# A retention kernel fused with an act-snake feed-forward layer: the first chunks interleaved, and work moved between GpSimd, VectorE and ScalarE

## The chip, the cores and the metric

The kernel runs on one core of a Trainium2 chip. The metric is the device time of one execution, in microseconds (us), and smaller is better. The runs shown of the kernel before are three, with a median of 246.03 us (245.74 to 247.08).

## What is computed

The reference has two steps. The first is a retention recurrence over q, k and v (batch 4, 8 heads, 768 positions, head width 64) with one decay `gamma` per head. The second takes the 3072 x 512 result x through a feed-forward layer of width 2048 with the activation h + sin(alpha h)^2 / alpha:

```python
for t in range(S):
    state = gamma * state + outer(k[t], v[t])
    y[t] = scale * q[t] @ state
x = y.transpose(0, 2, 1, 3).reshape(B * S, H * D)
h = x @ w_in
s = sin(alpha * h)
out = (h + s * s / (alpha + 1e-9)) @ w_out
```

## The kernel before, in words

**Tiling.** The recurrence is computed in 24 chunks of 128 positions (6 for each batch). A chunk j goes through four steps. `scale_v` (L163) multiplies v by decay powers `kg` into a new tile `vs`. `stage_T` (L168) transposes q and k on TensorE (PE) with eight transposes into the PSUM tile `pt`, and copies them to SBUF as `qkT`. `stage_A` (L181) makes the 128 x 128 products of k and q for the eight heads in the PSUM tile `pa`, and VectorE (DVE) multiplies them with a causal mask into `aT`. `stage_M` (L193), called the mix below, adds the product of the carried state `s_bd` and q to that of `vs` and `aT` in the PSUM tile `py`; DVE multiplies `py` with the decay table `qg` of the chunk's place into `xT` (L220), and ScalarE (ACT) copies the new state `ps` into `s_bd` (L224).

**Groups.** The 24 chunks form seven groups of 3, 2, 4, 4, 4, 4 and 3. For a group, `phase` (L309) runs through the 16 blocks f of the feed-forward width. `ff_in` (L229) multiplies block f of `w_in` with the group's `xT` into a PSUM tile `ph`; ACT takes the sine (L238); the square is made by ACT, DVE or GpSimd (POOL), by a pattern of the letters A, D and P (L240, L243); and DVE joins square and `ph` into `gT` (L244). Into the same loop are written, by hand, the steps T, A and M of the next group's chunks (the table `att`, by f) and the products of the group before with `w_out` (`ff_out`, L250, which accumulates 16 blocks in a PSUM tile `po`, copies it out at L262 and stores it). Below, phase 0 to phase 6 are these loops.

**Order.** The schedule is manual: each engine carries out its instructions in the order in which the program names them. All loads but three go through POOL's queue, cast from float32 to bfloat16 on the way. The program issues 14 of them ahead (L113), and the others one or three at a time out of the `att` tables. Between them POOL's queue has the decay tables (L149), `scale_v` from chunk 3 on (L165), and the squares of letter P (L243). The first q and k come in float32 through the sync engine's queue and are cast on DVE (L285, L286).

**PSUM.** There are eight banks. Four belong to the tag `mm` (`ph`, `po`, `scratch` and `pal`), two to `pa`, one to `ps`, and one to the tag `ty`, which `pt` and `py` share: the transposes of a chunk wait until `xT` of the chunk before has been read out of it.

**The start.** Before phase 0 the chunks 0, 1 and 2 run one after the other (L285 to L306), with matmuls on a tile of zeros (`idle_work`, L275) in the gaps. In `stage_T` with `split` the q half is copied by ACT (L175) and the k half by DVE (L176).

Of the kernel before, what the change touches and what calls it, by code (L numbers as in the profile page):

```python
# [15 lines left out]
def kernel(  # L16
# [56 lines left out]

    WP = 4
# [45 lines left out]
    mask01 = consts.tile([128, 128], BF16, name="mask01")  # L120
    nc.vector.tensor_scalar(mask01, tio, pos[:, 0:1], None, op0=ALU.is_ge)
    mask_bc = mask01[:, None, :].to_broadcast([128, H, 128])


# [6 lines left out]
    kg = consts.tile([128, NCH, H], F32, name="kg")  # L131
    nc.scalar.activation(out=kg, in_=expo, func=ACTF.Exp, scale=-1.0)

    lgp = consts.tile([128, NP], F32, name="lgp")
    for p in range(NP):
        for e in range(2):
            nc.vector.memset(lgp[64 * e:64 * e + 64, p:p + 1], lng[2 * p + e])
    qg = consts.tile([128, NCH, NP, C], F32, name="qg")
    for p in range(NP):
        nc.scalar.activation(out=qg[:, 0, p, :], in_=tio, func=ACTF.Exp, scale=lgp[:, p:p + 1])  # L140
    step = consts.tile([128, NCH, NP], F32, name="step")
    for c in range(1, NCH):
        nc.scalar.activation(out=step[:, c, :], in_=lgp, func=ACTF.Exp, scale=float(C * c))
    for name in "qk":
        raw[name, 0] = big.tile([128, H, D], BF16, name=f"{name}b")
    nc.vector.tensor_scalar_mul(qg[:, 0], qg[:, 0], scale)

    def decay_table(c, eng):
        eng.tensor_mul(qg[:, c], qg[:, 0], step[:, c, :, None].to_broadcast([128, NP, C]))  # L149


    s_bd = [big.tile([128, NP, 128], BF16, name=f"s_bd{i}") for i in range(2)]
    for t in s_bd:
        nc.vector.memset(t, 0.0)
# [178 lines left out]
    def L(n):  # L333
        return lambda: issue(n)
# [79 lines left out]
```

## Time and profile before

| | before |
|---|---|
| median of the runs | 246.03 us |
| the profiled execution's own time | 248.4 us |
| its span, first to last instruction | 246.4 us |
| PE busy | 217.8 us (88%) |
| DVE busy | 156.6 us (64%) |
| ACT busy | 148.1 us (60%) |
| POOL busy | 97.3 us (39%) |

Busy time is the time in which an engine works on an instruction; PEld is TensorE's loading of weights, which lies beside its matmuls. A row of a timeline gives start, duration, engine, line, operation and tiles, how many instructions were merged, and in brackets the idle time before it with what ended it. "PEclk" is the granted TensorE clock as a share of 2.4 GHz: 0.50 is the lower of its two levels, 1.2 GHz. A granted clock of 1.00 is also shown for stretches in which TensorE does nothing or has only begun.

### The profile page before, as it was taken

Reading aid. Unit: us, or ns where it says so; the run is one execution under the profiler, and the core shown is the slowest. Engines: PE = TensorE matmul, PEld = TensorE weight load, DVE = VectorE, ACT = ScalarE, POOL = GpSimd, SP = SyncE. Lnnn points to the kernel's source line nnn. Section 1 sums busy time; section 2 is a strip of 40 time slices with the busy share of each in tenths; the row PEclk is TensorE's granted clock in tenths of the full one; section 3 lists DMA queues with packets and bytes.
Section 4 is the critical chain, followed back from the end, with each engine's and each line's share of the span. In section 5 each row is a group of like instructions: output and inputs, shape, how many; then the busy total and the mean of one; then the engine's idle time right before and its main releaser. Section 6 shows DMA issues by size and latency. Waiting matters only on the chain.

```text
span 246.4 us, 4382 instructions
## 1 busy us (share of the span) xinstructions
PE 217.8 (88%) x1728; PEld 115.3 (47%) x1755; DVE 156.6 (64%) x247; ACT 148.1 (60%) x272; POOL 97.3 (39%) x112
## 2 busy tenths in 40 slices
PE   6786975798879989699999799999799999999993
PEld 2344543455654545344554444545444554555441
DVE  5655596458994787737766756876674776455420
ACT  5323985164547878557676576667567776777500
POOL 8993199999999965650301300110000000000000
PEclk9659999799999999889999999999999999999999
DMA  9999999999999998991041011101101110111122
GB/s 131 160 204 177 196 198 130 107 108 98 179 139 152 106 118 60 59 147 48 0 64 45 0 47 43 43 3 43 45 0 43 47 43 0 43 45 43 43 85 85
DMA packets 82611, 20.46 MB, mean 83 GB/s; under 512 B 75408, under 2 KB 79520, under 8 KB 82592
## 3 DMA queue, kind: packets, MB, share of 16 engines
q0 software_dynamic: 77024, 13.37, 69.1%
q1 hardware_dynamic: 5568, 6.83, 7.9%
q8 instruction: 13, 0.21, 0.4%
q14 instruction: 6, 0.05, 0.1%
HBM read 27.27 MB, written 6.29 MB: 136 GB/s over the span
## 4 chain that ended last, share of the span: by engine, by line
PE 73%; DVE 9%; POOL 6%; ACT 4%; DMA 4%; issue 3%; SPq 0%; DVEq 0%; ACTq 0%
PE po L253 31%; PE ph L235 29%; PE pt L172 4%; PE pa L187 3%; DVE aT L190 3%; DVE xT L220 3%; ACT s L238 2%; DMA k<-in_k_dram 2%; DMA kr<-in_k_dram 2%; PE py L204 2%; PE py L208 2%; PE scratch L277 2%; DVE gT L244 1%; POOL qr L71 1%; ACT s L240 1%
## 5 line engine op out<-in xcount | busy, mean ns | idle before, releaser
L244 DVE SCALAR_TENSOR_TENSOR gT<-s,rec_alpha,ph 128x512 bf16<-128x512 f32 (+2 forms) x112 | 74.4, 669 | 62.6 <-ACT s L240 59.2
L235 PE MATMUL ph<-xT,w_in 128*128 128x512 bf16 (+2 forms) x446 | 101.1, 352 | 5.6 <-DVE gT L244 3.2
L238 ACT ACTIVATE s<-ph,alpha_sb 128x512 f32<-128x512 f32 (+2 forms) x112 | 69.7, 625 | 53.4 <-PE ph L235 53.4
L253 PE MATMUL po<-w_out,gT 128*128 128x512 bf16 x361 | 96.5, 383 | 2.5 <-issue 1.6
L235 PEld LDWEIGHTS <-w_in 128*128 128x128 bf16 x448 | 43.8, 98 | 51.7 <-issue 9.4
L240 ACT ACTIVATE s<-s 128x512 f32<-128x512 f32 (+2 forms) x102 | 59.0, 578 | 3.2
L253 PEld LDWEIGHTS <-gT 128*128 128x128 bf16 x384 | 35.3, 98 | 34.4 <-issue 1.1
L165 POOL TENSOR_TENSOR vs<-vr,kg 128x512 bf16<-128x512 bf16 x21 | 22.6, 1076 | 57.3 <-PE ps L217 32.0
L190 DVE TENSOR_TENSOR aT<-pa,mask 128x1024 bf16<-128x1024 f32 x24 | 29.3, 1222 | 2.6 <-PE pa L187 2.4
L224 ACT CAST s_bd<-ps 64x256 bf16<-64x256 f32 x40 | 14.5, 362 | 20.6 <-PE ps L217 20.1
L71 POOL DMA_DIRECT2D vr<-in_v_dram x24 | 22.4, 934 | 0.2 <-issue 0.2
L71 POOL DMA_DIRECT2D kr<-in_k_dram x23 | 21.2, 920 | 0.0
L71 POOL DMA_DIRECT2D qr<-in_q_dram x23 | 21.0, 912 | 0.0
L220 DVE TENSOR_TENSOR xT<-py,qg 128x512 bf16<-128x512 f32 x24 | 16.4, 684 | 6.2 <-PE py L208 6.2
L262 DVE COPY o_sb<-po 128x512 f32<-128x512 f32 x23 | 15.7, 684 | 4.7 <-PE po L253 4.7
L178 DVE COPY qkT<-pt 128x1024 bf16<-128x1024 bf16 x21 | 14.5, 689 | 1.4 <-PE pt L172 0.9
L187 PE MATMUL pa<-qkT 64*128 64x128 bf16 x192 | 10.0, 226 | 5.2 <-DVE qkT L178 3.6
L187 PEld LDWEIGHTS <-qkT 64*128 64x128 bf16 x192 | 5.6, 97 | 15.3 <-issue 6.6
L208 PE MATMUL py<-aT,vs 128*64 128x128 bf16 x192 | 10.2, 230 | 2.9 <-DVE xT L220 1.8
L277 PE MATMUL scratch<-warm 128*128 128x512 bf16 x24 | 10.0, 555 | 1.6 <-DVE warm L117 1.2
L204 PE MATMUL py<-qkT,s_bd 128*64 128x128 bf16 x160 | 8.7, 233 | 2.9 <-DVE xT L220 2.9
L172 PE MATMUL pt<-ident,qr 128*128 128x128 bf16 x92 | 9.1, 222 | 1.6 <-DVE xT L220 1.3
(52 smaller groups left out, 87.7 us busy)
## 6 DMA issues: line engine op xcount, KB each, us to landing
out_dram<-o_sb SPq DMA_DIRECT2D x24, 256.0 KB, 2.0
vr<-in_v_dram POOLq DMA_DIRECT2D x24, 128.0 KB, 4.3
qr<-in_q_dram POOLq DMA_DIRECT2D x23, 128.0 KB, 4.4
kr<-in_k_dram POOLq DMA_DIRECT2D x23, 128.0 KB, 4.5
w_in<-in_moe_w_in_dram POOLq DMA_DIRECT2D x4, 512.0 KB, 9.2
w_out<-in_moe_w_out_dram POOLq DMA_DIRECT2D x4, 512.0 KB, 11.3
q<-in_q_dram SPq DMA_DIRECT2D x1, 256.0 KB, 3.2
k<-in_k_dram SPq DMA_DIRECT2D x1, 256.0 KB, 4.9
```

The costliest lines, as they stand in the source:

```text
L71: nc.gpsimd.dma_start(out=t, in_=chunk_of(src, j))
L165: eng.tensor_mul(vs, raw["v", j], kg[:, j % NCH, :, None].to_broadcast([128, H, D]))
L172: nc.tensor.transpose(pt[:, i * NP + p, :], t[:, 2 * p:2 * p + 2, :].rearrange("p h d -> p (h d)"), ident)
L187: nc.tensor.matmul(pa[:, e, p, :], qkT[r, NP + p, :], qkT[r, p, :], start=(p == 0), stop=True, skip_group_check=True)
L190: nc.vector.tensor_mul(aT.rearrange("p e n t -> p (e n) t"), pa.rearrange("p e n t -> p (e n) t"), mask_bc)
L220: nc.vector.tensor_mul(xT[g][:, :, o:o + C], py, qg[:, c])
L235: nc.tensor.matmul(ph, w_in[:, i, f * 128:(f + 1) * 128], xT[g][:, i, :], start=(i == 0), stop=(i == KS - 1))
L238: nc.scalar.activation(out=s, in_=ph, func=ACTF.Sin, scale=alpha_sb[:, f:f + 1])
L240: nc.scalar.activation(out=s, in_=s, func=ACTF.Square)
L244: return lambda: nc.vector.scalar_tensor_tensor(gT[g][:, f, :], s, rec_alpha[:, f:f + 1], ph, op0=ALU.mult, op1=ALU.add)
L253: nc.tensor.matmul(po[g, ts], gT[g][:, f, ts * C:(ts + 1) * C], w_out[:, f, :], start=(f == 0), stop=(f == FF - 1))
L262: nc.vector.tensor_copy(o_sb, po[g, ts])
```

## The change

In the order of the diff:

- All loads are issued by POOL in one go, in the same order as before, with nothing between them up to chunk 10. `scale_v` of chunks 9 to 23 stays on POOL, each behind the loads two chunks later. `scale_v` of chunks 0 to 8 and the decay tables go to DVE, and no square is left on POOL. `scale_v` writes in place, into the loaded v.
- The transposes of chunks 0, 1 and 2 go into banks of the tag `mm`, and those of chunk j + 1 stand ahead of the mix of chunk j. There are 37 `idle_work` matmuls instead of 26.
- The whole `qkT` copy is ACT's (chunk 0 in two halves), and so are the `o_sb` copies, but for half of the last.
- The squares go by AAD in phases 0 and 2, by AAAD in the others. Before they went by AADAAPADA in phase 0, AAD in phase 1, and A from phase 2 on.
- In phase 0 the mix of chunk 3 moves behind the loop, and from phase 2 on T, A and M of the next group stand one or two blocks earlier; its last M is at f = 14 instead of 15.

The core of the diff, with setup lines that only change places left out:

```diff
     def scale_v(j, eng):
-        vs = work.tile([128, H, D], BF16, name="vs", tag="vs", bufs=5)
-        eng.tensor_mul(vs, raw["v", j], kg[:, j % NCH, :, None].to_broadcast([128, H, D]))
-        st["vs", j] = vs
+        eng.tensor_mul(raw["v", j], raw["v", j], kg[:, j % NCH, :, None].to_broadcast([128, H, D]))
...
-    def stage_T(j, split=False):
-        pt = psum.tile([128, 2 * NP, 128], BF16, name="pt", tag="ty")
...
+    def open_T(j, tag="ty", bufs=1):
+        st["pt", j] = psum.tile([128, 2 * NP, 128], BF16, name="pt", tag=tag, bufs=bufs)
...
+    def stage_T(j):
+        open_T(j)
+        half_T(j, 0)
+        half_T(j, 1)
+        nc.scalar.copy(st["qkT", j], st["pt", j])
...
-                nc.vector.tensor_copy(o_sb, po[g, ts])
+                nc.scalar.copy(o_sb, po[g, ts])
...
+    LATE = 9
+    todo = [lambda j=j: load_chunk(j) for j in (1, 2)]
+    todo += [lambda i=i: load_w_in(i) for i in range(3)]
+    todo += [lambda: load_chunk(3), lambda: load_w_in(3), lambda: load_chunk(4)]
+    todo += [lambda i=i: load_w_out(i) for i in range(WP)]
+    todo += [lambda j=j: load_chunk(j) for j in range(5, LATE)]
+    for j in range(LATE, NJ):
+        todo += [lambda j=j: load_chunk(j)]
+        if j > LATE + 1:
+            todo += [lambda j=j: scale_v(j - 2, nc.gpsimd)]
...
-    idle_work(8)
+    idle_work(9)
     nc.vector.tensor_copy(raw["q", 0], near["q"])
+    open_T(0, "mm", 4)
+    half_T(0, 0)
+    nc.scalar.copy(st["qkT", 0][:, :NP, :], st["pt", 0][:, :NP, :])
+    nc.vector.tensor_scalar_mul(qg[:, 0], qg[:, 0], scale)
+    decay_table(1)
+    idle_work(6)
     nc.vector.tensor_copy(raw["k", 0], near["k"])
+    half_T(0, 1)
+    nc.scalar.copy(st["qkT", 0][:, NP:, :], st["pt", 0][:, NP:, :])
     scale_v(0, nc.vector)
-    stage_T(0, True)
-    idle_work(2)
+    idle_work(4)
     stage_A(0)
...
-    idle_work(4)
-    stage_M(0)
-    for j in range(1, groups[0]):
-        scale_v(j, nc.vector)
-        stage_T(j, True)
-        decay_table(j, nc.gpsimd)
-        idle_work(2)
-        stage_A(j)
-        idle_work(4)
-        stage_M(j)
+    open_T(1, "mm", 4)
+    half_T(1, 0)
+    half_T(1, 1)
+    nc.scalar.copy(st["qkT", 1], st["pt", 1])
+    scale_v(1, nc.vector)
+    for t in s_bd:
+        nc.vector.memset(t, 0.0)
+    idle_work(3)
+    stage_M(0)
+    idle_work(1)
+    stage_A(1)
+    open_T(2, "mm", 4)
+    half_T(2, 0)
+    idle_work(2)
+    half_T(2, 1)
+    nc.scalar.copy(st["qkT", 2], st["pt", 2])
+    scale_v(2, nc.vector)
     nc.tensor.transpose(pal, alpha_row, ident_f)
+    idle_work(3)
+    stage_M(1)
+    idle_work(1)
+    stage_A(2)
     nc.scalar.copy(alpha_sb, pal)
+    sin0 = consts.tile([128, 1], F32, name="sin0")
+    nc.scalar.activation(out=sin0, in_=warm[:, 0:1], func=ACTF.Sin)
+    decay_table(2)
     nc.vector.tensor_scalar_add(rec_alpha, alpha_sb, 1e-9)
     nc.vector.reciprocal(rec_alpha, rec_alpha)
...
+    idle_work(5)
+    stage_M(2)
+    idle_work(3)
...
-    phase(0, [], att, "AADAAPADA")
+    phase(0, [], {2: [G(3)], 5: [G(4)], 9: [T(3), V(3)], 11: [A(3)], 13: [G(5)]}, "AAD")
     outs = out_pieces(0)
     stage_T(4)
+    scale_v(4, nc.vector)
     for fn in outs[:4]:
         fn()
     stage_A(4)
+    stage_M(3)
     for fn in outs[4:8]:
         fn()
     stage_M(4)
...
-    phase(1, outs[8:], att, "AAD")
+    phase(1, outs[8:], {7: [T(5), V(5)], 8: [A(5)], 9: [T(6), V(6)], 10: [A(6), M(5)], 11: [T(7), V(7)],
+                        12: [A(7), M(6)], 13: [T(8), V(8)], 14: [A(8), M(7)]}, "AAAD")
     stage_M(8)
...
             for i, j in enumerate(js):
-                a = int(i * step_f)
-                att.setdefault(a, []).extend([L(3), V(j)])
-                att.setdefault(a + 1, []).append(T(j))
-                att.setdefault(a + 3, []).append(A(j))
+                a = i * FF // len(js)
+                att.setdefault(max(a - 1, 0), []).append(T(j))
+                att.setdefault(a + 1, []).append(A(j))
                 if i > 0:
-                    att[a + 3].append(M(j - 1))
-            att.setdefault(FF - 1, []).append(M(js[-1]))
-        phase(g, out_pieces(g - 1), att, "A")
+                    att[a + 1].append(M(j - 1))
+            att.setdefault(FF - 2, []).append(M(js[-1]))
+        phase(g, out_pieces(g - 1), att, "AAD" if g == 2 else "AAAD")
```

## Rows read from the trace of the kernel before

**Rows 1.** Windows by stage: length; busy PE, PEld, DVE, ACT, POOL; PEclk; DMA share, GB/s

```profile
0.00:23.73 23.73, 16.43 (x138) 8.07 (x141) 13.83 (x40) 8.72 (x23) 19.37 (x28) 0.78 1.55 168
23.73:47.78 24.05, 17.45 (x152) 10.04 (x153) 16.50 (x25) 15.23 (x32) 17.91 (x20) 0.95 1.67 161
47.78:74.17 26.39, 22.75 (x245) 14.97 (x248) 20.89 (x36) 14.43 (x34) 26.39 (x30) 0.98 1.76 129
74.17:103.57 29.40, 26.52 (x236) 14.00 (x240) 20.93 (x29) 22.54 (x38) 21.90 (x25) 0.99 1.31 99
103.57:140.28 36.71, 34.96 (x284) 17.95 (x288) 24.01 (x33) 23.80 (x41) 9.24 (x11) 0.96 0.47 54
140.28:175.16 34.88, 33.13 (x270) 17.15 (x273) 23.88 (x33) 23.04 (x38) 2.46 (x3) 1.00 0.08 31
175.16:207.65 32.49, 32.23 (x239) 16.08 (x241) 21.31 (x30) 22.31 (x36) 0.00 (x0) 1.00 0.09 34
207.65:246.40 38.75, 34.36 (x172) 17.02 (x174) 15.27 (x25) 18.02 (x33) 0.00 (x0) 1.00 0.15 55
```

**Rows 2.** Timeline of the start: start us, us, engine, line, operation [idle before <-releaser]

```profile
4.94 0.41 DVE L285 CAST qb<-q 128x512 bf16<-128x512 f32 x1
...
6.18 0.90 DVE L286 CAST kb<-k 128x512 bf16<-128x512 f32 x1 [0.83 <-DMA k<-in_k_dram]
...
9.32 1.22 DVE L190 TENSOR_TENSOR aT<-pa,mask 128x1024 bf16<-128x1024 f32 x1 [0.71 <-PE pa L187]
...
11.92 0.69 DVE L220 TENSOR_TENSOR xT<-py,qg 128x512 bf16<-128x512 f32 x1 [0.82 <-PE py L208]
...
12.53 1.02 DVE L165 TENSOR_TENSOR vs<-vr,kg 128x512 bf16<-128x512 bf16 x1
12.67 0.58 PE L172 MATMUL pt<-ident,qr 128*128 128x128 bf16 x4 [0.58 <-DVE xT L220]
...
13.72 0.58 ACT L175 COPY qkT<-pt 128x512 bf16<-128x512 bf16 x1 [0.82 <-PE pt L172]
...
22.98 0.69 DVE L220 TENSOR_TENSOR xT<-py,qg 128x512 bf16<-128x512 f32 x1 [0.57 <-PE py L208]
```

**Rows 3.** Timelines of phase 0's end: one row of POOL, one of DVE

```profile
41.58 0.88 POOL L243 TENSOR_TENSOR s<-s 128x384 f32<-128x384 f32 x1
...
42.50 1.14 DVE L244 SCALAR_TENSOR_TENSOR gT<-s,rec_alpha,ph 128x384 bf16<-128x384 f32 x2 [2.41 <-POOL s L243]
```

**Rows 4.** Timelines of PE at the ends of phases 2 and 3

```profile
102.37 0.41 PE L208 MATMUL py<-aT,vs 128*64 128x128 bf16 x8 [1.76 <-DVE xT L220]
...
103.57 1.86 PE L235 MATMUL ph<-xT,w_in 128*128 128x512 bf16 x4
...
138.71 0.41 PE L204 MATMUL py<-qkT,s_bd 128*64 128x128 bf16 x8 [1.23 <-DVE xT L220]
```

**Rows 5.** Groups by line and shape: busy us, mean ns of one | idle before

```profile
L244 DVE SCALAR_TENSOR_TENSOR gT<-s,rec_alpha,ph 128x512 bf16<-128x512 f32 x64 | 47.7, 746 | 39.9 <-ACT s L240 39.8
L238 ACT ACTIVATE s<-ph,alpha_sb 128x512 f32<-128x512 f32 x64 | 44.0, 687 | 35.5 <-PE ph L235 35.5
...
L240 ACT ACTIVATE s<-s 128x512 f32<-128x512 f32 x64 | 40.3, 630 | 2.0
...
L71 POOL DMA_DIRECT2D vr<-in_v_dram x24 | 22.4, 934 | 0.2 <-issue 0.2
...
L178 DVE COPY qkT<-pt 128x1024 bf16<-128x1024 bf16 x21 | 14.5, 689 | 1.4 <-PE pt L172 0.9
```

**Rows 6.** Timelines of DVE's squares, and of POOL beside the second

```profile
27.30 0.55 DVE L243 TENSOR_TENSOR s<-s 128x384 f32<-128x384 f32 x1
...
31.71 1.50 DVE L243 TENSOR_TENSOR s<-s 128x384 f32<-128x384 f32 x1
...
64.28 1.09 DVE L243 TENSOR_TENSOR s<-s 128x256 f32<-128x256 f32 x1
...
31.40 1.05 POOL L149 TENSOR_TENSOR qg<-qg,step 128x512 f32<-128x512 f32 x1
```

More of the change, by code (lines that the diff above doesn't have):

```diff
@@ L72, in load, with load_chunk @@
         raw[name, j] = t
+    def load_chunk(j):
+        for name, src in (("q", q), ("k", k), ("v", v)):
+            load(name, src, j)
     WP = 4
@@ L119 @@
     nc.vector.tensor_scalar(ident, tio, pos[:, 0:1], None, op0=ALU.is_equal)
-    mask01 = consts.tile([128, 128], BF16, name="mask01")
-    nc.vector.tensor_scalar(mask01, tio, pos[:, 0:1], None, op0=ALU.is_ge)
-    mask_bc = mask01[:, None, :].to_broadcast([128, H, 128])
+    lgp = consts.tile([128, NP], F32, name="lgp")
+    for p in range(NP):
+        for e in range(2):
+            nc.vector.memset(lgp[64 * e:64 * e + 64, p:p + 1], lng[2 * p + e])
     lg = consts.tile([128, H], F32, name="lg")
@@ L140 @@
         nc.scalar.activation(out=qg[:, 0, p, :], in_=tio, func=ACTF.Exp, scale=lgp[:, p:p + 1])
+    kg = consts.tile([128, NCH, H], F32, name="kg")
+    nc.scalar.activation(out=kg, in_=expo, func=ACTF.Exp, scale=-1.0)
     step = consts.tile([128, NCH, NP], F32, name="step")
@@ L143, with decay_table @@
         nc.scalar.activation(out=step[:, c, :], in_=lgp, func=ACTF.Exp, scale=float(C * c))
[L144 to L154, printed above, removed]
+    def decay_table(c):
+        nc.vector.tensor_mul(qg[:, c], qg[:, 0], step[:, c, :, None].to_broadcast([128, NP, C]))
+    mask01 = consts.tile([128, 128], BF16, name="mask01")
+    nc.vector.tensor_scalar(mask01, tio, pos[:, 0:1], None, op0=ALU.is_ge)
+    mask_bc = mask01[:, None, :].to_broadcast([128, H, 128])
+    ident_f = consts.tile([FF, FF], F32, name="ident_f")
+    nc.vector.tensor_copy(ident_f, ident[:FF, :FF])
     alpha_sb = consts.tile([128, FF], F32, name="alpha_sb")
     rec_alpha = consts.tile([128, FF], F32, name="rec_alpha")
+    s_bd = [big.tile([128, NP, 128], BF16, name=f"s_bd{i}") for i in range(2)]
     st = {}
@@ L273, with idle_work @@
+    todo += [lambda j=j: scale_v(j, nc.gpsimd) for j in (NJ - 2, NJ - 1)]
+    for fn in todo:
+        fn()
     scratch = psum.tile([128, 512], F32, name="scratch", tag="mm", bufs=4)
-    def idle_work(n):
+    pal = psum.tile([128, FF], F32, name="pal", tag="mm", bufs=4)
+    def idle_work(n, w=512):
         for _ in range(n):
-            nc.tensor.matmul(scratch, warm[:, :128], warm, start=True, stop=True)
-    idle_work(8)
-    pal = psum.tile([128, FF], F32, name="pal", tag="mm", bufs=4)
@@ L281 @@
-    ident_f = consts.tile([FF, FF], F32, name="ident_f")
-    nc.vector.tensor_copy(ident_f, ident[:FF, :FF])
-    nc.vector.tensor_copy(raw["q", 0], near["q"])
+            nc.tensor.matmul(scratch[:, :w], warm[:, :128], warm[:, :w], start=True, stop=True)
+    idle_work(9)
+    nc.vector.tensor_copy(raw["q", 0], near["q"])
+    open_T(0, "mm", 4)
[3 more added lines that the diff above has]
+    decay_table(1)
@@ L328, in M, with V, G @@
         return lambda: stage_M(j)
[L330 to L344 removed]
+    def V(j):
+        return lambda: scale_v(j, nc.vector)
+    def G(c):
+        return lambda: decay_table(c)
+    phase(0, [], {2: [G(3)], 5: [G(4)], 9: [T(3), V(3)], 11: [A(3)], 13: [G(5)]}, "AAD")
     outs = out_pieces(0)
     stage_T(4)
+    scale_v(4, nc.vector)
     for fn in outs[:4]:
```

66 lines of the change are left out of this document (9 added, 57 removed).

## The prediction

> **What bounds the kernel now.** I read the busy time by stage first [rows 1]. A stage runs from the first `ph` matmul of a phase to that of the next. The reader is to compare the length of a stage with the time that PE was busy in it. In phases 5 and 6 and the last products (the last two rows) PE is the bound: 32.23 of 32.49 us in phase 5. Before that there are gaps: 7.3 us in the start, 6.6 in phase 0, 3.6 in phase 1, 2.9 in phase 2, 1.75 each in phases 3 and 4. In the start and in phase 0 PE's busy time is filler too, or stretched by a granted clock of 0.78 and 0.95. So the later stages can give little, the early ones much.
>
> The timeline of the start [rows 2] shows why it is long. The transposes of chunk 1 at 12.67 had waited for `xT` of chunk 0 (11.92), as both use the `ty` bank. A chunk is one serial loop through all engines: transposes, a copy by ACT (0.58), one by DVE, the products, `aT` (1.22), the mix, `xT` (0.69). From 11.92 to 22.98 two chunks took 11.06 us, 5.5 each.
>
> At the end of phase 0 [rows 3] a square on POOL began only at 41.58, behind POOL's loads, and DVE stood idle for 2.41 us. At the ends of phases 2 and 3 [rows 4] the last mix waits 1.76 and 1.23 us for the `xT` of the mix before it, and after the first of these waits four 512-column `ph` matmuls took 1.86 us: the lower clock level.
>
> **The change part by part.** I take the stages in order, with the span of the profiled execution (246.4 us; its own time is 248.4). That execution is 2.4 us above the median of 246.03, so I use differences, and take them off the median.
>
> *Start, 23.7 us before.* The cast of k (6.18 to 7.08) still waits for the load of k, which stays first in its queue. Behind it come transposes, copy, products and `aT` of chunk 0 as before; `scale_v` and the clearing of `s_bd` now fall between `aT` and `xT`, so the first `xT` still ends near 12.3. But then the transposes and the `qkT` copy of the next chunk are done in other banks beside the `aT` before, and leave the loop. What is left for a chunk is DVE's own work, `aT` 1.22, `xT` 0.69 and `scale_v` 1.02 [rows 2], which also hides a mix and the products on PE only in part: I add 0.5 us, 3.4 in all. 12.3 + 2 x 3.4 is 19.1, and 19.2 with the handoff to PE. Two things can lengthen it. One is the decay tables on DVE, of which no row exists: above zero, below POOL's 1.05 for the same shape [rows 6], and nearest to DVE's own 384-column square of 0.55, which in proportion is 0.73. Table 1 is covered by the wait for k, tables 2 to 5 are not. The other is the filler: 37 matmuls instead of 26, at 0.47 us each if the clock is at its lower level as in the 1.86 us row [rows 4]; five stand before the mix of chunk 2 (2.3 us against an `aT` of 1.22). So 18.5 to 21.5. Gain: 4.5.
>
> *Phase 0, 24.05 us.* The 2.41 us of waiting for POOL [rows 3] goes. DVE becomes what is late next: from 16.50 us busy it loses two `qkT` copies of 0.69 [rows 5], gains two squares, three tables and two `scale_v` (2 x 0.55 + 3 x 0.73 + 2 x 0.7, that is 4.7), and comes to 19.8; ACT gets two copies and comes to some 17.2. The copy of all 1024 columns on ACT has no row: it costs at least the 0.58 of 512 columns [rows 2], at most twice that. I take 1.0, near the upper end, as only the fixed part is saved. Behind the loop the `qkT` copy, products, `aT`, two mixes and two `xT` of chunks 3 and 4 form a chain that now starts behind ACT's last square and holds the mix of chunk 3 as well. That takes back 0.5. I take 22.2 (21 to 24). Gain: 1.9.
>
> *Phase 1, 26.39 us.* Here PE (22.75), DVE and ACT come near each other. DVE goes from 20.89 to about 19 (four `qkT` and two `o_sb` copies out, four `scale_v` in), ACT from 14.43 to about 20. PE's share of lower clock at the beginning goes; waits between the three stay. I take 25.2 (24 to 26.4). Gain: 1.2.
>
> *Phase 2, 29.40 us.* The last mix stands one block earlier and its products two, so the 1.76 us wait is covered by `ph` and `po` matmuls of the last two blocks. ACT goes from 22.54 to 22.54 + 4 x 1.0 + 2 x 0.6 - 5 x 0.63, that is 24.6: close under PE's 26.5. I take 28.0 (27.2 to 29.4). Gain: 1.4.
>
> *Phases 3 and 4, 36.71 and 34.88 us.* Phase 3 loses the lower clock (a mean of 0.96 over 36.71 us is 1.5 us of work lost [rows 1]) and most of its 1.23 us wait; phase 4 most of its like wait. ACT goes from 23.80 to 23.80 + 4 x 1.0 + 4 x 0.6 - 4 x 0.63, that is 27.7 of 34. I take 34.1 and 33.9. Gain: 2.6 and 1.0.
>
> *Phases 5 and 6 and the end:* nothing, as PE has no gap there; the copies that move to ACT lie beside PE's matmuls.
>
> *POOL.* A chunk with `scale_v` costs POOL three issues of 0.93 [rows 5] and about 1.05, together 3.9 us. From phase 2 on, PE uses a chunk in more than 7 us. The loads stand in the same order as before, none later than before; so they cost nothing. If this cover goes, PE waits for a chunk. A `scale_v` on POOL that waits for its v holds up the loads behind it, but never one that its own v is behind.
>
> The sum: 4.5 + 1.9 + 1.2 + 1.4 + 2.6 + 1.0 = 12.6. 246.03 - 12.6 is 233.4 us (the profiled execution's own time would be 235.8).
>
> One row speaks of a price that I leave out of the sum. DVE's square of 384 columns took 0.55 us at 27.30, and 1.50 at 31.71, where POOL had begun a decay table at 31.40 and held it to 32.45 [rows 6]. With POOL's arithmetic gone from the early stages that delay goes. But the square of 256 columns at 64.28 took 1.09, and the cast of k 0.90 where that of q took 0.41 [rows 2], while POOL only issued loads. The Trainium skill, page "SBUF — State Buffer", section "Who interferes with whom", says that a DVE instruction with two SBUF inputs contends only with a GpSimd instruction that reads SBUF, and that casts and copies contend with descriptor generation too. By that the squares, tables and `scale_v` on DVE would be undisturbed and the sum stands; by the row at 64.28 they are not always. The row decides that it must be a rival.
>
> **The rivals.**
> 1. *The start is no shorter.* DVE's order, not the `ty` bank, sets the loop, or the lower clock level stretches the filler. For it: the start now holds more DVE work behind one another, and more filler. Against: the transposes waited for `xT` in the rows. The start keeps 23.7, and the time is 233.4 + 4.5, about 238.
> 2. *POOL's loads block DVE.* 25 squares, tables, casts and `scale_v` stand on DVE up to the end of phase 1, while POOL issues loads. If each costs 0.5 us more (the two rows above: 0.49 for the cast, over 0.5 for the square), 12.5 us come on DVE, of which all but some 2 us is on the path: about 244. Against: the square at 27.30 paid nothing, though POOL was quiet just then.
> 3. *Slower: ACT holds the `mm` banks.* An `o_sb` copy now queues on ACT behind a sine of 0.69, a square of 0.63 [rows 5] and sometimes a `qkT` copy, and its bank of `po` comes free that much later. With four banks PE then waits for one. 23 such copies at 0.7 us are 16 us, which turns the gain of 12.6 into a loss: about 249. It decides from 0.55 us a copy. Against: three banks leave three blocks of `ph` and `po`, over 3 us, for a sine, a square and `gT` (0.69 + 0.63 + 0.75), and ACT is under 85% busy in phases 3 to 6.
> 4. *The change doesn't do what it says* would be that the tile of a bank is handed over late, so that the early transposes still wait; it is rival 1 in its time.
>
> **How the numbers follow.** The forecast has 0.74, rival 1 (with 4) 0.14, rivals 2 and 3 0.06 each. The bounds of the start, of phases 0 to 2 reach from 2.9 us below the sum to 6.7 above it if all fall together; I take 230 to 238 for the forecast. With rival 1 the range is 230 to 239.5, and little more than rivals 2 and 3 is left out. A measurement of this kernel tells about 0.5% (1.2 us) from no change. Half of rival 2 may be eaten up (0.03), and rival 3 has 0.01 within the bound: faster 0.91, same 0.04, slower 0.05.
>
> **What would show it.** In the changed profile the first `ph` matmul should start near 19 us (rival 1: 23 or more), that of phase 1 near 41.5, of phase 2 near 66.5, of phase 3 near 94.5. The transposes of chunk 1 should stand before the mix of chunk 0 and wait for loads or PE alone. The squares on DVE should have one length each by width (rival 2: two). `ph` should wait for no `o_sb` (rival 3: a wait on the ACT copy in every phase). The granted clock should stay at 1.00 from phase 1 on. The prediction is wrong if PE has new gaps in phases 2 to 6, or if DVE works without a pause through phase 0 and 1 and still ends late.

## The result, and the profile after

The changed kernel takes 234.68 us (median of four runs, 233.82 to 235.32), beside 245.88 (245.53 to 247.08) for the kernel before. The ratio is 0.9534, with a 95% interval of 0.9488 to 0.9580: faster by 11.2 us, where 12.6 had been forecast. (A run more than 1.5% above the fastest of its kernel is left out of ratios and medians here and below; e3, e5 and e7 have one each.) The profiled execution has a span of 233.0 us and an own time of 234.89.

The windows by stage of the changed kernel stand against [rows 1]; columns are the same, and each stage again begins with the first `ph` of a phase. (The line numbers from here on are those of the kernel whose rows are shown.)

```profile
0.00:17.45 17.45, 15.49 (x148) 8.09 (x151) 12.91 (x39) 10.22 (x24) 14.49 (x22) 1.00 1.47 157
17.45:39.26 21.81, 16.57 (x152) 9.57 (x152) 17.77 (x30) 16.88 (x33) 10.69 (x13) 1.00 1.65 189
39.26:64.55 25.29, 22.62 (x245) 14.66 (x249) 18.13 (x32) 20.05 (x42) 22.44 (x26) 1.00 2.37 150
64.55:93.34 28.79, 26.68 (x236) 13.95 (x240) 21.28 (x28) 23.04 (x38) 28.79 (x32) 1.00 1.74 126
93.34:127.60 34.26, 33.46 (x284) 17.37 (x288) 21.36 (x28) 26.90 (x45) 7.96 (x9) 1.00 0.46 55
127.60:161.52 33.92, 33.38 (x268) 17.02 (x272) 21.53 (x28) 26.01 (x43) 0.00 (x0) 1.00 0.09 32
161.52:194.09 32.57, 32.03 (x237) 16.00 (x240) 19.86 (x26) 24.73 (x40) 0.00 (x0) 1.00 0.09 33
194.09:233.00 38.91, 34.58 (x174) 17.12 (x175) 13.93 (x23) 20.08 (x37) 0.00 (x0) 0.98 0.15 55
```

The reader is to see that the start and phase 0 are shorter with nearly the same work in them, and that phases 3 and 4 end close to PE's busy time (33.46 of 34.26, 33.38 of 33.92). Their gaps are gone, and so is the lower clock that phase 3 had. In phase 2 a gap of 2.1 us is left.

Four groups of the changed kernel were prices of the prediction (busy time, mean ns of one, idle before):

```profile
L161 ACT COPY qkT<-pt 128x1024 bf16<-128x1024 bf16 x21 | 21.0, 1000 | 0.7 <-PE pt L154 0.7
L243 ACT COPY o_sb<-po 128x512 f32<-128x512 f32 x23 | 13.5, 590 | 8.1 <-PE po L234 8.1
L146 DVE TENSOR_TENSOR vr<-vr,kg 128x512 bf16<-128x512 bf16 x9 | 6.2, 685 | 0.0
L130 DVE TENSOR_TENSOR qg<-qg,step 128x512 f32<-128x512 f32 x5 | 3.4, 685 | 0.1
```

The timeline of the start (start, duration, engine, line, tiles; in brackets the idle time before) shows the new loop:

```profile
5.43 1.98 PE L274 MATMUL scratch<-warm 128*128 128x512 bf16 x6
5.55 0.88 DVE L285 CAST kb<-k 128x512 bf16<-128x512 f32 x1
...
7.25 0.39 PE L154 MATMUL pt<-ident,kb 128*128 128x128 bf16 x4
...
8.76 0.40 PE L154 MATMUL pt<-ident,qr 128*128 128x128 bf16 x4
...
10.15 0.41 PE L190 MATMUL py<-aT,vr 128*64 128x128 bf16 x8
...
11.16 0.63 DVE L202 TENSOR_TENSOR xT<-py,qg 128x512 bf16<-128x512 f32 x1
...
13.85 0.69 DVE L202 TENSOR_TENSOR xT<-py,qg 128x512 bf16<-128x512 f32 x1 [0.34 <-PE py L190]
...
16.77 0.63 DVE L202 TENSOR_TENSOR xT<-py,qg 128x512 bf16<-128x512 f32 x1
...
17.45 0.81 PE L217 MATMUL ph<-xT,w_in 128*128 128x384 bf16 x4 [0.24 <-DVE xT L202]
```

The transposes of chunk 1 (8.76) stand ahead of the mix of chunk 0 (10.15) and wait for nothing. From one `xT` to the next it is 2.69 and 2.92 us; before it was 6.33 and 4.73 (11.92, 18.25, 22.98), and 4.73 twice in the second profile of the kernel before (e4 below).

### The profile page after: what moved, and what is told of

The parts are those of the page before. It is cut to its first block, busy times and chain, and to the rows that moved or that the text cites. A ratio compares the mean times of both kernels' runs of the same rounds, so it can differ in the third digit from the quotient of the medians.

```text
span 233.0 us, 4372 instructions
## 1 busy us (share of the span) xinstructions
PE 214.8 (92%) x1737; PEld 113.8 (49%) x1766; DVE 146.8 (63%) x233; ACT 167.9 (72%) x297; POOL 84.4 (36%) x99
## 4 chain that ended last, share of the span: by engine, by line
PE 72%; DVE 16%; ACT 7%; issue 3%; DVEq 0%; ACTq 0%
PE po L234 31%; PE ph L217 27%; DVE aT L172 5%; DVE gT L225 4%; PE scratch L274 4%; ACT s L220 3%; PE pt L154 3%; PE pa L169 3%; DVE xT L202 3%; ACT qkT L161 3%; DVE s L224 2%; PE py L186 2%; PE py L190 2%; ACT s L222 1%; DVE qg L130 1%
## 5 line engine op out<-in xcount | busy, mean ns | idle before, releaser
L217 PE MATMUL ph<-xT,w_in 128*128 128x512 bf16 (+2 forms) x444 | 99.5, 348 | 6.0 <-DVE gT L225 3.5
L234 PE MATMUL po<-w_out,gT 128*128 128x512 bf16 x361 | 95.4, 379 | 2.2 <-issue 1.4
L222 ACT ACTIVATE s<-s 128x512 f32<-128x512 f32 (+2 forms) x82 | 46.6, 568 | 2.6
L224 DVE TENSOR_TENSOR s<-s 128x512 f32<-128x512 f32 (+2 forms) x30 | 19.5, 651 | 9.4 <-ACT s L220 9.4
L71 POOL DMA_DIRECT2D kr<-in_k_dram x23 | 20.4, 889 | 4.7 <-DMA w_out<-in_moe_w_out_dram 3.2
L161 ACT COPY qkT<-pt 128x1024 bf16<-128x1024 bf16 x21 | 21.0, 1000 | 0.7 <-PE pt L154 0.7
L243 ACT COPY o_sb<-po 128x512 f32<-128x512 f32 x23 | 13.5, 590 | 8.1 <-PE po L234 8.1
L146 POOL TENSOR_TENSOR vr<-vr,kg 128x512 bf16<-128x512 bf16 x15 | 16.2, 1083 | 3.9 <-ACT s L222 2.1
L274 PE MATMUL scratch<-warm 128*128 128x512 bf16 x35 | 11.5, 462 | 1.4 <-DVE warm L105 1.2
L190 PE MATMUL py<-aT,vr 128*64 128x128 bf16 x192 | 9.5, 220 | 0.5 <-DVE xT L202 0.4
```

Source lines behind the costliest of these rows:

```text
L71: nc.gpsimd.dma_start(out=t, in_=chunk_of(src, j))
L161: nc.scalar.copy(st["qkT", j], st["pt", j])
L217: nc.tensor.matmul(ph, w_in[:, i, f * 128:(f + 1) * 128], xT[g][:, i, :], start=(i == 0), stop=(i == KS - 1))
L222: nc.scalar.activation(out=s, in_=s, func=ACTF.Square)
L224: (nc.vector if square == "D" else nc.gpsimd).tensor_mul(s, s, s)
L234: nc.tensor.matmul(po[g, ts], gT[g][:, f, ts * C:(ts + 1) * C], w_out[:, f, :], start=(f == 0), stop=(f == FF - 1))
```

## The experiments

The runs were made on several chips, and on each the kernel before was timed too (medians 245.88 to 246.8), so kernels are compared by their ratios to it. "The changed kernel" is at 0.9534. The runs have the labels e1 to e12.

### The kernel before, profiled again (e4)

The code is unchanged; this is a second profiled execution of it.

> The kernel before once more, for a second profile of it. The span shrank by 13.4 us between the two profiles but the median only by 11.2 us, and the profiled execution of before is 2.4 us over its median. If the first profile caught an execution with more of the lower clock than usual, this one shows a span of 243.5 to 245 us and fewer slices below a granted clock of 1.00. If it is the profile itself, the span is again 246.4 within 0.5 us.

It took 246.7 us, with a span of 244.9. Its window for the start, and its cast of k:

```profile
0.00:20.93 20.93, 15.04 (x140) 7.21 (x141) 13.40 (x40) 8.72 (x23) 17.87 (x26) 1.00 1.69 165
```

```profile
5.37 0.84 DVE L286 CAST kb<-k 128x512 bf16<-128x512 f32 x1
```

The same instructions took 20.93 us in the start, not 23.73. The difference has two parts. In the first profile the cast of k waited 0.83 us for its load and began at 6.18 [rows 2], here at 5.37 without a wait, and the transposes of k came 0.9 us earlier (6.26 instead of 7.14). From them to the first `ph` it took 14.67 us instead of 16.59: in the first profile more of the start ran at the lower clock (four transposes of chunk 1 took 0.58 us at 12.67 [rows 2], here 0.38 at 11.46). So 2.8 us of the start that I had worked from belonged to that execution, 0.9 by a later load and 1.9 by the clock. The waits at the ends of phases 0, 2 and 3 are there again, with the same lengths (2.41, 1.76, 1.23). All stages in us:

| stage | before | before, again | forecast | after |
|---|---|---|---|---|
| start | 23.73 | 20.93 | 19.2 | 17.45 |
| phase 0 | 24.05 | 24.77 | 22.2 | 21.81 |
| phase 1 | 26.39 | 26.84 | 25.2 | 25.29 |
| phase 2 | 29.40 | 29.40 | 28.0 | 28.79 |
| phase 3 | 36.71 | 36.90 | 34.1 | 34.26 |
| phase 4 | 34.88 | 34.87 | 33.9 | 33.92 |
| phase 5 | 32.49 | 32.33 | 32.5 | 32.57 |
| phase 6 and end | 38.75 | 38.86 | 38.75 | 38.91 |

### The start in the old order (e1)

```diff
-    open_T(1, "mm", 4)
-    half_T(1, 0)
-    half_T(1, 1)
-    nc.scalar.copy(st["qkT", 1], st["pt", 1])
...
+    for j in range(1, groups[0]):
+        scale_v(j, nc.vector)
+        stage_T(j)
+        if j == 2:
+            decay_table(2)
+        idle_work(2)
+        stage_A(j)
+        idle_work(4)
+        stage_M(j)
```

> The changed kernel, with only the start put back into serial order: chunks 1 and 2 are scaled, transposed, multiplied and mixed one after the other, and the transposes use the ty bank again. Filler, loads, copies and later phases are those of the change. If the gain of the start (6.3 us between the two traces) comes from transposes and copy leaving the serial loop, the first ph matmul goes back from 17.5 to 22 us or more, and the time is 4.5 to 6 us above the changed kernel's (239 to 241). Rival: the gain of the start comes from other things (the clock, which no longer falls, the decay tables and loads): then the start lengthens by less than 2 us and the time stays under 237.

Measured: 238.63 us (237.74 to 238.98), ratio 0.9703 (0.9642 to 0.9763): 4 us slower than the changed kernel, a little under what I expected. Its timeline shows the old wait:

```profile
15.34 0.69 DVE L202 TENSOR_TENSOR xT<-py,qg 128x512 bf16<-128x512 f32 x1 [0.50 <-PE py L190]
16.08 0.38 PE L154 MATMUL pt<-ident,qr 128*128 128x128 bf16 x4 [0.66 <-DVE xT L202]
...
19.96 0.69 DVE L202 TENSOR_TENSOR xT<-py,qg 128x512 bf16<-128x512 f32 x1 [0.50 <-PE py L190]
20.71 0.48 PE L217 MATMUL ph<-xT,w_in 128*128 128x384 bf16 x2 [0.66 <-DVE xT L202]
```

A chunk is 4.62 us there, and the first `ph` comes at 20.71: 3.3 us later than in the changed kernel, and where the kernel before had it in its second profile (20.93). The old order with its shared bank takes the whole gain of the start away; the next run parts the two.

### The old bank, the new order (e2)

```diff
-    open_T(0, "mm", 4)
+    open_T(0)
```

and the same for chunks 1 and 2.

> The changed kernel, with the transposes of chunks 0 to 2 in the ty bank that they share with the mix, in the new order. If it is the order that counts, the mix of chunk 0 waits a little for the copy of chunk 1 and the transposes of chunk 2 wait for the first xT: 0.5 to 1.5 us more than the changed kernel. If it is the spare banks that count, 3 us or more.

Measured: 236.29 us (234.62 to 237.03), ratio 0.9593 (0.9531 to 0.9656), which overlaps the changed kernel's interval; the two ratios are 0.6% (1.5 us) apart. The profiled execution is the fastest of the four (234.62 us), and its first `ph` stands at 17.46, as in the changed kernel's profile. But its transposes of k stood at 6.47, where the changed kernel's stood at 7.25. From there to the first `ph` it took 10.99 us; in six profiles with the changed kernel's start code it is 10.17 to 10.61. The waits for the shared bank can be seen on PE:

```profile
9.71 0.41 PE L190 MATMUL py<-aT,vr 128*64 128x128 bf16 x8 [0.45 <-ACT qkT L294]
...
11.07 0.38 PE L154 MATMUL pt<-ident,qr 128*128 128x128 bf16 x4 [0.17 <-DVE xT L202]
```

These are the two waits that I had expected, and 0.4 to 0.8 us is their price in this profile. The new order gives most of the start's gain, the spare banks little. The old order with spare banks was not run.

### One filler matmul instead of 37 (e3)

```diff
-    idle_work(9)
+    idle_work(1)
...
-    idle_work(4)
```

and all the others in the start taken out.

> The changed kernel with 1 filler matmul in the start instead of 37. If the filler is what keeps the granted clock at 1.00 through the start, the clock falls to 0.50 for some of the start and perhaps of phase 0, and the time is 1 to 3 us longer. Rival: the transposes, products and mixes keep the clock alone, or the lower clock is hidden by DVE's chain; then the time is the same within 0.5 us, or up to 0.6 us shorter, since the first transposes wait for the ninth filler matmul (5.01 against the cast's end at 4.50).

Measured: 234.48 us (233.5 to 235.71), ratio 0.9533 (0.9461 to 0.9604): no difference. PE of this kernel in the start:

```profile
6.69 0.61 PE L154 MATMUL pt<-ident,kb 128*128 128x128 bf16 x4 [1.51 <-DVE kb L284]
...
17.06 1.44 PE L217 MATMUL ph<-xT,w_in 128*128 128x384 bf16 x4 [0.66 <-DVE xT L202]
```

Four transposes take 0.61 us all through the start, against 0.39 in the changed kernel: the lower clock level, though the column of the granted clock has 1.00 here. Still the first `ph` comes at 17.06, and from the transposes of k to it 10.37 us pass, where the changed kernel took 10.20. So the filler and the clock that it keeps up decide little here: the lower level costs 0.2 us on this path. I read the equal times as the one paying for the other, which is not shown by itself. That the filler can be on the path is seen in the changed kernel's own profiles: its six matmuls ahead of the transposes of k took 1.98 us (at 5.43, above), while the cast of k had ended at 6.43, so the transposes came 0.8 us late. Run e9 below has the same start; there the six took 1.46 us from 4.89, the transposes of k stood at 6.49, and the first `ph` at 16.67. In six profiles with this start code the first `ph` stands between 16.65 and 17.96.

### The old places of T, A and M in phases 2 to 5 (e5)

```diff
-                a = i * FF // len(js)
-                att.setdefault(max(a - 1, 0), []).append(T(j))
-                att.setdefault(a + 1, []).append(A(j))
+                a = int(i * (FF / len(js)))
+                att.setdefault(a + 1, []).append(T(j))
+                att.setdefault(a + 3, []).append(A(j))
                 if i > 0:
-                    att[a + 1].append(M(j - 1))
-            att.setdefault(FF - 2, []).append(M(js[-1]))
+                    att[a + 3].append(M(j - 1))
+            att.setdefault(FF - 1, []).append(M(js[-1]))
```

> The changed kernel with T, A and M of the next group back at their old places in phases 2 to 5 (the last mix at f = 15). If the gains at the phase ends come from the places, the waits of the last mix for xT return in phases 2, 3 and 4 (1.2 to 1.8 us each), with a spell of the lower clock after the longest: 3 to 5 us more than the changed kernel (237.5 to 239.5). Rival: the squares and copies that moved between ACT and DVE gave these gains; then less than 1.5 us more.

Measured: 242.61 us (242.26 to 244.92), ratio 0.9865 (0.9806 to 0.9924): by the ratios 8 us slower than the changed kernel, about twice what I expected. Phases 2 to 5 take 138.03 us in the profile instead of 129.54, and more than in the kernel before (133.50 in its second profile). (Phase 1, which the edit leaves alone, took 27.21 us here instead of 25.29; see the last section.) DVE and PE at the end of phase 3:

```profile
127.80 0.69 DVE L224 TENSOR_TENSOR s<-s 128x512 f32<-128x512 f32 x1 [0.32 <-ACT s L220]
128.41 1.22 DVE L172 TENSOR_TENSOR aT<-pa,mask 128x1024 bf16<-128x1024 f32 x1
129.54 0.68 DVE L202 TENSOR_TENSOR xT<-py,qg 128x512 bf16<-128x512 f32 x1
```

```profile
130.27 0.41 PE L186 MATMUL py<-qkT,s_bd 128*64 128x128 bf16 x8 [2.21 <-DVE xT L202]
...
132.43 1.91 PE L217 MATMUL ph<-xT,w_in 128*128 128x512 bf16 x4
```

The wait that was 1.23 us at this place [rows 4] is 2.21, and behind it matmuls run at the lower level (1.91 for four `ph`, 1.03 in the changed kernel). The reason stands in DVE's rows: by the new pattern AAAD the square of block 15 is DVE's, and in the old places `aT` and `xT` of the last mixes queue behind it. The end of phase 2 is the control: there the pattern AAD leaves the square of block 15 to ACT, and the wait is 1.82 us, much as the 1.76 before. The places and the pattern belong together.

### All squares of phases 2 to 6 on ACT (e8)

```diff
-        phase(g, out_pieces(g - 1), att, "AAD" if g == 2 else "AAAD")
+        phase(g, out_pieces(g - 1), att, "A")
```

> The changed kernel with all squares of phases 2 to 6 on ACT, as before the change, while the copies stay on ACT. If ACT has become close to the bound (26.9 of 34.3 us busy in phase 3, 23.0 of 28.8 in phase 2), 5 x 0.63 more in phase 2 lengthens it by 1 to 2 us and phases 3 to 6 by 0 to 1 us each: 2 to 4 us more in all. If PE alone sets these phases, within 0.7 us.

Measured: 235.0 us, ratio 0.9528 (0.9502 to 0.9554). The rival holds: phases 2 to 5 take 129.83 us, the changed kernel's 129.54. In the new places the split of the squares does nothing.

### The copies back to DVE (e6)

```diff
-        nc.scalar.copy(st["qkT", j], st["pt", j])
+        nc.vector.tensor_copy(st["qkT", j], st["pt", j])
...
-                nc.scalar.copy(o_sb, po[g, ts])
+                nc.vector.tensor_copy(o_sb, po[g, ts])
```

> The changed kernel with the qkT copies of chunks 3 to 23 and the o_sb copies back on DVE; squares and places are those of the change. If PE is the bound from phase 2 on whoever copies, phases 3 to 6 keep their length within 0.3 us and the time is within 1 us of the changed kernel; phase 0 and 1 tell which engine is late there: if DVE, 0.5 to 1.5 us more, if ACT, 0.5 to 1 us less. If the copies had to leave DVE for the gain, 3 us more or worse.

Measured: 236.02 us, ratio 0.9561 (0.9528 to 0.9594): level with the changed kernel within the intervals, by two effects that partly cancel. Its windows for phase 1, and for phases 2 to 5 together, and one row of DVE in phase 1:

```profile
39.38:67.53 28.15, 22.78 (x244) 14.66 (x248) 23.04 (x39) 14.63 (x35) 26.95 (x30) 1.00 2.35 151
67.53:195.58 128.05, 125.54 (x1021) 64.39 (x1040) 99.48 (x137) 81.11 (x135) 33.07 (x36) 1.00 0.51 57
```

```profile
57.15 1.65 DVE L146 TENSOR_TENSOR vr<-vr,kg 128x512 bf16<-128x512 bf16 x1
```

Phase 1 is 2.9 us longer (25.29), with DVE at 23.04 us busy instead of 18.13, and phase 0 is 0.4 longer; phases 2 to 5 are 1.5 us shorter (129.54). So what I expected if DVE is the late engine, 0.5 to 1.5 us more, was too little. Not all of the 2.9 us is the copies': a `scale_v` took 1.65 us where 0.68 is usual, DVE then worked without a pause to the next `xT`, and PE waited 1.63 us for that one instead of 0.47. That is about 1 us, which leaves some 1.9 for the copies. ACT is the better place for them in phase 1, and the worse one after it.

### The copies on ACT in phases 0 and 1 only (e9)

```diff
+        (nc.scalar.copy if j < 9 else nc.vector.tensor_copy)(st["qkT", j], st["pt", j])
...
+                (nc.scalar.copy if g < 1 else nc.vector.tensor_copy)(o_sb, po[g, ts])
```

> The changed kernel, but from phase 2 on (chunks 9 to 23, output groups from 1 on) the qkT and o_sb copies go back to DVE; in phases 0 and 1 they stay on ACT. Theory (the copies on ACT pay in phase 1, where DVE is the fuller engine, and cost a little from phase 2 on): phases 0 and 1 keep their 21.8 and 25.3 us, phases 2 to 5 take about 128 us together instead of 129.5, the time falls by 1 to 1.5 us, to 233.2 to 233.7. Rival (which engine copies makes no difference in the late phases, PE sets them): 234.7 within 0.7.

Measured: 232.8 us (232.37 to 232.92), ratio 0.9431 (0.9402 to 0.9460), clear of the changed kernel's interval and some 1% faster than it. Its windows for phases 2 to 4:

```profile
63.75:91.62 27.87, 26.69 (x236) 13.96 (x240) 24.36 (x33) 19.17 (x32) 27.87 (x31) 1.00 1.75 127
91.62:125.64 34.02, 33.39 (x284) 17.41 (x288) 25.88 (x36) 21.64 (x37) 8.17 (x9) 1.00 0.47 56
125.64:159.33 33.69, 33.32 (x269) 17.02 (x273) 25.97 (x36) 20.42 (x35) 0.00 (x0) 1.00 0.09 32
```

Phases 0 and 1 keep their 21.80 and 25.28; phase 2 falls from 28.79 to 27.87, phases 3 and 4 by 0.24 and 0.23. Phases 2 to 5 take 128.24 us together, as expected, which is 1.3 us of gain; the rest of the 2.1 us between the two profiled spans is mostly the start (16.67 against 17.45), whose code is the same. This version beats both kernels.

### DVE's idle slot in the start filled (e10)

As the run before, and:

```diff
     scale_v(0, nc.vector)
+    for t in s_bd:
+        nc.vector.memset(t, 0.0)
+    decay_table(2)
     idle_work(4)
```

(both taken from their later places).

> As the run before, and the clearing of s_bd and decay table 2 are put into DVE's idle 1.8 us of the start, between scale_v of chunk 0 and the first aT. Theory (the start is a chain of DVE's work): the first ph of phase 0 comes some 0.7 to 1.2 us earlier, at 16.3 to 16.8 instead of 17.45, and the time falls by as much, to about 232.5. Rival (the start is set by PE's filler and the clock): the first ph stays at 17.4 and the time is that of the run before.

Measured: 232.8 us, ratio 0.9433 (0.9404 to 0.9463), the same as the run before; the first `ph` stands at 16.87. The theory is refuted, and the rival has the time right. From the transposes of k it took 9.87 us (7.00 to 16.87) instead of 10.18 (6.49 to 16.67), so 0.3 us were won at most. `xT` of chunk 1 still waits for PE:

```profile
13.60 0.69 DVE L202 TENSOR_TENSOR xT<-py,qg 128x512 bf16<-128x512 f32 x1 [0.64 <-PE py L190]
```

The new start is a loop through PE and DVE, not a chain of DVE's work alone. That PE's filler sets it, as the rival had it, is not shown (e3).

### The mix of chunk 3 back in phase 0's loop (e11)

As the run before, and:

```diff
-    phase(0, [], {2: [G(3)], 5: [G(4)], 9: [T(3), V(3)], 11: [A(3)], 13: [G(5)]}, "AAD")
+    phase(0, [], {2: [G(3)], 5: [G(4)], 9: [T(3), V(3)], 11: [A(3)], 12: [V(4)], 13: [M(3), T(4)], 15: [A(4)]}, "AAD")
```

with table 5 in phase 1.

> As the run before, and at the end of phase 0 the mix of chunk 3 goes back into the loop (f = 13) and the transposes and products of chunk 4 with it (f = 13 and 15), decay table 5 goes to phase 1. Theory (behind the loop a chain of copy, products, aT and two mixes holds PE, its gaps there were 0.48, 0.63 and 0.66 us beside little other work): phase 0 takes 20 to 21 us instead of 21.8, and the time falls by another 1 to 1.5, to about 231. Rival (the added DVE work in the last blocks delays the last gT as much): phase 0 stays at 21.8 within 0.4.

Measured: 234.82 us (232.52 to 235.98), ratio 0.9510 (0.9468 to 0.9553): slower by 2 us than the run that it is built on, so both expectations missed. Phase 0 takes 23.42 us, phase 1 26.32. PE at the end of phase 0:

```profile
30.90 0.41 PE L190 MATMUL py<-aT,vr 128*64 128x128 bf16 x8 [1.14 <-DVE aT L172]
...
33.15 0.58 PE L154 MATMUL pt<-ident,qr 128*128 128x128 bf16 x4 [1.71 <-DVE xT L202]
...
33.95 2.61 PE L217 MATMUL ph<-xT,w_in 128*128 128x384 bf16 x8
```

The mix waits for `aT`, and the transposes of chunk 4 in the shared bank for `xT`, with `ph` of the next blocks behind both on PE; after 2.9 us of waiting eight `ph` take 2.61 us, 0.33 each, where twenty took 3.55, 0.18 each, at the start of phase 0. In phase 1 a `scale_v` of 1.54 and one of 1.36 beside POOL's come on top. The change is right to have this mix behind the loop, as far as these places tell.

### The kernel before with phase 0 without POOL's squares (e7)

```diff
-    phase(0, [], att, "AADAAPADA")
+    phase(0, [], att, "AAD")
```

> The kernel before with one edit: the squares of phase 0 go by AAD, so that none is on POOL. If the 2.41 us wait of DVE for POOL's last square was the loss of phase 0, phase 0 shortens by 1.5 to 2.5 us and with it the time, to 243.5 to 244.5. Rival: POOL's queue is late in any case (scale_v of chunk 4 began only at 44.17, behind loads, and is needed for the mix of chunk 4): then the wait moves there and the time falls by less than 1 us.

Measured: 243.36 us (241.69 to 243.57), ratio 0.9849 (0.9803 to 0.9896): 3 to 4 us, somewhat more than I expected. This one line brings over a quarter of what the whole change brings. PE behind phase 0, first in the kernel before, then here:

```profile
44.30 0.40 PE L187 MATMUL pa<-qkT 64*128 64x128 bf16 x8 [3.07 <-DVE qkT L178]
```

```profile
43.24 0.40 PE L187 MATMUL pa<-qkT 64*128 64x128 bf16 x8 [1.17 <-DVE qkT L178]
```

DVE's wait of 2.41 us for POOL is gone. PE's wait for the `qkT` copy behind it falls by 1.9 us, and what follows it runs at the upper clock level: eight matmuls of the mix take 0.41 us, in the kernel before 0.64. The forecast shortening of phase 0 can't be read from this profile, which is of the execution of 246.83 us: phase 0 took 23.45 us in it. Another wait came in there: a square took 2.40 us while POOL multiplied, and PE waited 2.16 us behind it:

```profile
26.34 2.40 DVE L243 TENSOR_TENSOR s<-s 128x384 f32<-128x384 f32 x1
```

### POOL multiplies later (e12)

```diff
-    LATE = 9
+    LATE = 13
```

with `scale_v` of chunks 9 to 12 on DVE.

> The changed kernel, but chunks 9 to 12 have their scale_v on DVE too, so that POOL has no arithmetic until the loads of chunk 13 and after. Theory (a DVE instruction with two SBUF inputs is stretched only while POOL does a multiplication): until POOL's first scale_v no square, table or scale_v on DVE is longer than 0.8 us, phase 1 takes its 25.3 us or up to 0.4 less, phase 2 has four times 0.69 more on DVE but no stretch, the time is 234.7 within 0.7. Rival (the loads that POOL issues stretch them): single DVE instructions of over 1.2 us appear in phases 0 and 1 all the same.

Measured: 235.32 us, ratio 0.9526 (0.9490 to 0.9562): the changed kernel's time, as expected. Phase 1 takes 25.28 us. POOL's first multiplication starts at 64.10, and no square, table or `scale_v` on DVE is over 0.8 us until then; afterwards four are, of which these three:

```profile
72.36 1.17 DVE L146 TENSOR_TENSOR vr<-vr,kg 128x512 bf16<-128x512 bf16 x1
...
75.74 1.28 DVE L224 TENSOR_TENSOR s<-s 128x512 f32<-128x512 f32 x1
...
87.81 1.53 DVE L146 TENSOR_TENSOR vr<-vr,kg 128x512 bf16<-128x512 bf16 x1
```

So the rival is refuted for this kernel, and here the theory holds for when stretching begins. Two other profiles, of the kernel before and of e7, speak against it. DVE's `scale_v` of chunk 1 took 1.02 us in the first (12.53, [rows 2]) and 1.45 in the second (at 11.94), though POOL only issued loads until its first multiplication at 14.09 in both. Nor does the theory cover the last row here: POOL's multiplication (86.25 to 87.33 in its timeline) had ended 0.5 us before, and it was issuing loads. Spans on POOL are rough in the profile.

## Why the prediction was right, and where its steps were off

**The time and the sum.** The measured gain of 11.2 us is 1.4 below the sum of 12.6, inside the range. Against the second profile of before, whose clock in the start was the higher one, the terms are: start 3.5 (4.5 forecast), phase 0 3.0 (1.9), phase 1 1.5 (1.2), phase 2 0.6 (1.4), phase 3 2.6 (2.6), phase 4 0.95 (1.0), the rest -0.3; together 11.9, of which I take the difference to 11.2 as the scatter of single executions. That the sum came so near is in part luck: the start gave 1.0 us less than forecast and phase 2 0.8 less, phase 0 1.1 more. One sum of the range was wrong: the lower bounds of the start and of phases 0 to 2 lie 0.7, 1.2, 1.2 and 0.8 us below the terms, which is 3.9 together and not 2.9.

**The start: right mechanism, mis-sized.** The length of 19.2 was too long and the gain of 4.5 too large at once. The first is mostly a term of the loop: 3.4 us a chunk had `scale_v` at the 1.02 us of one row [rows 2] and 0.5 for the mix; measured are 0.68 for `scale_v` and 2.7 to 2.9 for the loop. That one row was itself stretched: the two other `scale_v` of DVE in the same start took 0.67 and 0.68 us (at 7.00 and 18.86). The first `xT` ended at 11.79, for 12.3. The second is the base: 23.73 us held 2.8 us, of a later load of k and of lower clock, that the median of the runs need not hold (e4). I had noted that the profiled execution was 2.4 us above the median, and taken differences off the median all the same; the stage in which the 2.4 us lay was one from which I took a difference. e1 measures order and banks together: 3.3 us in the profile, 4 in the times. The spare banks, which my text named beside the order ("in other banks beside"), are 0.4 to 0.8 us of it in the profile of e2, and the filler's price of 0.47 each did not decide (e3).

**Phase 0.** The 2.41 us wait is gone, and e7 shows that taking the squares off POOL brings 3 to 4 us by itself. I had priced the wait alone; behind it PE's matmuls had run at the lower level too, a term that I left out. DVE came to 17.77 us busy and not 19.8, in part because the 16.50 that I started from held the square of 1.50 us [rows 6]. What the chain behind the loop costs (0.5 in the sum) no run shows by itself; e11, which takes it away, loses for other reasons.

**Phase 1: right.** 25.29 for 25.2. e6 shows that here the copies on ACT earn some 2 us, as DVE with them was busy for as long (23.04 us) as PE (22.78).

**Phase 2: the one step that failed.** I took 28.0 because places one or two blocks earlier cover the last mix, and noted ACT at 24.6 "close under PE's 26.5" without charging it. The rows of the changed kernel, PE first:

```profile
67.91 0.40 PE L169 MATMUL pa<-qkT 64*128 64x128 bf16 x8 [0.60 <-ACT qkT L161]
...
90.42 0.41 PE L190 MATMUL py<-aT,vr 128*64 128x128 bf16 x8 [0.36 <-DVE xT L202]
...
93.34 1.02 PE L217 MATMUL ph<-xT,w_in 128*128 128x512 bf16 x4 [0.55 <-DVE xT L202]
```

PE waits for the `qkT` copy on ACT, which stands behind a sine and a square, and at the end for `xT`, behind a square on DVE that was stretched to 1.75 us (row below). e9 gives the size of the first: when the copies leave ACT the wait of 0.60 is gone, PE's waits for `xT` before a `ph` fall from 1.4 to 1.1 us, and phase 2 takes 27.87 us, 0.92 less and close to the 28.0. The stretched square is no part of that: e9 has one too (1.50 us at 89.47). So nothing was wrong with the places; the copies' new queue on ACT was.

**Phases 3 and 4: right,** 34.26 and 33.92 for 34.1 and 33.9. e5 bears out that the places are what closes the waits, and that a wait there costs twice, by itself and by the lower clock behind it. What I had not seen is that the squares' new pattern makes the old places worse than they were (2.21 us of wait for 1.23 in phases 3 and 4). The pattern itself adds nothing (e8).

**The unknown prices** came out at 1.00 us for ACT's copy of 1024 columns (1.0 taken), 0.685 for a decay table on DVE (0.73), 0.59 for `o_sb` on ACT (0.6).

**The rivals.** Rival 1 (start no shorter) and 4 (the early transposes still wait) fell with the first `ph` at 17.45. Rival 3 (ACT holds the `mm` banks) would show as `ph` or `po` waiting for `o_sb`; among PE's waits in the changed kernel none does (one weight load of the products waits 0.4 us for it, once). Rival 2 (POOL's loads block DVE) was wrong in its price of 0.5 us on each of 25 operations. In the changed kernel no square, table or `scale_v` on DVE exceeds 0.72 us until late in phase 2, though POOL is busy for half of phase 0 and most of phase 1 (10.69 and 22.44 us), nearly all of it with issuing loads; one then does, as POOL multiplies (one row of POOL, one of DVE):

```profile
90.56 1.08 POOL L146 TENSOR_TENSOR vr<-vr,kg 128x512 bf16<-128x512 bf16 x1
```

```profile
90.94 1.75 DVE L224 TENSOR_TENSOR s<-s 128x512 f32<-128x512 f32 x1
```

The 1.09 us at 64.28 in the kernel before, on which this rival rested [rows 6], stood 1.1 us behind a multiplication on POOL (62.07 to 63.15 in its timeline) and is of the same kind as the unsettled row of e12. The Trainium skill, page "SBUF — State Buffer", section "Who interferes with whom", has it that a DVE instruction with two SBUF inputs contends only with a GpSimd instruction that reads SBUF. The changed kernel's trace agrees as to loads: the seven `scale_v` on DVE ahead of POOL's first multiplication (53.70) took 0.68 or 0.69 us, six of them beside loads. The kernel before and e7 do not: one `scale_v` took 1.02 and 1.45 us beside loads alone, as said under e12. Nor do the traces show the end of the hold as sharply as the rule would have it. When a DVE instruction is stretched stays open. The cast of k is another matter: 0.88 us in the changed kernel, 0.42 in e11, with POOL issuing loads in both.

**The signs** that I named were mostly met: transposes of chunk 1 ahead of the mix of chunk 0, the granted clock of 1.00 from phase 1 to phase 5, phases 1 to 3 beginning at 39.26, 64.55 and 93.34 (41.5, 66.5 and 94.5 forecast, the difference being mostly the start's). Two were not: PE has a new wait in phase 2 (the 0.60 us above), and the squares have not one length each by width (the 1.75 us).

## What to carry to other kernels

When a gain is taken as a difference from a profiled execution that is slower than the median, look for the stage in which its surplus lies before you take a gain from that stage: here one start held 2.8 us that another execution of the same code did not. Check too whether the row that a price comes from is like its fellows. In a serial loop over several engines it is the order that pays, the next step's independent work ahead of the dependent step; check by itself what the extra buffers earn, and in what company a new pattern of engines puts the steps that end a stage. Which of two engines should copy is a matter of the stage: charge the copy to the queue that it joins wherever that engine is near the bound, and move it per stage.

## What the runs showed that I had not expected

One `scale_v` on DVE, 0.68 us elsewhere, took 3.19 us in e5, from 54.83 to 58.02, longer than POOL's multiplication inside it (55.65, 1.08 us) and itself together; the rest of that time POOL issued loads. Phase 1 of that execution is 1.9 us longer than the changed kernel's. These rows are from e5, DVE and POOL together:

```profile
54.83 3.19 DVE L146 TENSOR_TENSOR vr<-vr,kg 128x512 bf16<-128x512 bf16 x1
55.65 1.08 POOL L146 TENSOR_TENSOR vr<-vr,kg 128x512 bf16<-128x512 bf16 x1
```

And the column of the granted clock can say 1.00 while matmuls take half as long again or more (e3): in a start the durations of like matmuls tell more than it does.
